# Sorting the keys of two batches with full-width products: two positions per product, all columns at once

## The chip, the cores and the metric

The kernel runs on one core of a Trainium2 chip. The metric is the device time of one execution in microseconds. Five engines matter. TensorE (PE in the profile) multiplies, with its weight loads shown as PEld. VectorE (DVE) and ScalarE (ACT) move results out of PSUM, the memory that TensorE writes. GpSimd (POOL) and SyncE (SP) mostly start transfers. A profile row names the line of the kernel, the engine, the operation, and the tiles as output<-input.

## The reference, cut to what matters

There are 4 batches, 8 heads, 768 positions and 64 columns per head. The positions of a head form 8 blocks of 96. A small matrix `P` per head (8 by 8) is normalised in five rounds; then blocks of keys and values are mixed by it, attention is computed inside each block, and the result goes through a two-layer network.

```python
k_sorted = np.einsum('bhij,bhjcd->bhicd', P, k_b)      # block i = sum over j of P[i, j] * block j
v_sorted = np.einsum('bhij,bhjcd->bhicd', P, v_b)
scores = scale * np.matmul(q_b, k_sb.transpose(0, 1, 2, 4, 3))
attn = softmax(scores)                                  # within a block of 96
x = (attn @ v_sb)                                       # heads side by side: 512 columns per token
r = np.maximum(x @ w_in, 0.0)                           # 512 -> 2048
out = (s * r * r + b) @ w_out                           # 2048 -> 512
```

The change touches only how `k_sorted` is made for batches 2 and 3.

## The kernel before, in words

Everything is written out by hand for one instruction stream per engine; there is no scheduler that reorders. Batches are worked on in halves of 384 tokens, numbered `t` = 0 to 7 (two per batch). For each half the network is `ffn1` (L464: 16 groups of 128 hidden columns, taken in pairs by `part`, products at L460, ReLU on ScalarE, squaring on VectorE) and `ffn2` (L478: three groups `m` of 128 tokens, each of 16 products at L484, and a move out by `store` on VectorE, L505). The loop at L618 runs, for each batch `b`, ffn1 of its two halves and then ffn2 of its two halves. The attention of the next batch `n = b + 1` is threaded between these products: dictionaries of slots name the pieces, and a piece's instructions are issued right after the product of its slot. In `ffn2`, slot `m * 4 + f // 4` comes after each four products.

The keys of batch `n` are sorted in `k_piece` (L290). The raw keys lie in SBUF with a partition for each (head, block, half of the block), 128 of them for the four pairs of heads, and (48 positions, 64 columns) along it. The matrices `P` of the batch form one table `PD[b]` with dimensions (partition, e, z, g): `e` is which head of a pair, `z` which half of a block, `g` the pair and the block, so 2 x 2 x 32 = 128 columns. A product for one position `c` and one `e` takes the 128 x 64 raw keys as weights and 64 columns of `PD` as the moving operand, and writes 64 partitions (the columns `d` of the keys) of PSUM: `e` = 0 to partitions 0 to 63, `e` = 1 to 64 to 127. So the two products of a position use two halves of TensorE's columns. A piece does 16 positions (CK), 32 products, and one move (`evac`, L202) of 1024 elements per partition on VectorE ("D") or ScalarE ("A") puts it in `KS`, whose last dimension is the position. Three pieces make a batch.

For batches 2 and 3 the three pieces are issued at once in slot 0 of `ffn2(2b)`, that is after the first four products of the first token group:

```python
            s0 = {0: [K(n, 0, "D"), K(n, 1, "A"), K(n, 2, "D")]}
        s1 = {0: [SC(n, 0, 0), SC(n, 0, 1)],
```

Their first use is by the scores (`SC`, `s_piece`, L353) in slot 0 of `ffn2(2b + 1)`. Batches 0 and 1 sort their keys elsewhere, with `k_piece` and `k_banks`, and are not touched.

PSUM tiles come from two pools in turn: `psa` (3 buffers of two banks: `hps` of ffn1, the sorted keys `tp`, scores, `pv`) and `psb` (2 buffers of one bank: `ops` of ffn2 and others). A product that opens a new tile waits until the tile that had the buffer before has been moved out. In `ffn2` the group `m` = 2 therefore needs the buffer that `store` of `m` = 0 has read.

Three transfers run in the background during this time: the sorted values come back through DRAM into `VS` (`v_back`, L339), the queries are transposed into `QT` by two transposing transfers on SP's queue (`q_dma`, L439), and finished rows go out (`store`). POOL's queue loads the raw keys of batch `n` before, in six parts (`load`, L86).

Of the kernel before, what the change touches and what calls it, by code (L numbers as in the profile page):

```python
# [9 lines left out]
FP = mybir.dt.float32  # L10
# [12 lines left out]
def kernel(  # L23
# [12 lines left out]
    nc = tc.nc  # L36

    B, H, S, D = q.shape
# [12 lines left out]
    NG = NHP * NB  # L51
    VW = D + 2
    CK = 16
# [15 lines left out]
    psa = ctx.enter_context(tc.tile_pool(name="psa", bufs=3, space=bass.MemoryType.PSUM))  # L69
# [14 lines left out]
    RAW = {}  # L84
# [37 lines left out]
    KS = [const.tile([128, NG, 2, GAP], BF, name=f"ks{i}") for i in range(2)]  # L122
# [79 lines left out]
    def evac(eng, out, in_):  # L202
        if eng == "A":
            nc.scalar.copy(out=out, in_=in_)
        else:
            nc.vector.tensor_copy(out=out, in_=in_)  # L206

    def q_banks(b, half, engs):
# [3 lines left out]
        for u in range(2):  # L212
# [13 lines left out]
            out=jsel, in_=ident.rearrange("p (h j z) -> p j h z", h=H, j=NB), axis=AX.XY, op=ALU.add),  # L226
        lambda: nc.vector.tensor_reduce(
            out=bm.rearrange("p (e z a) -> p e z a", e=2, z=2),
# [26 lines left out]
    PD = {}  # L255
# [34 lines left out]
    def k_piece(b, c0, eng):  # L290
        ps = psa.tile([128, CK, 2, NG], FP, tag="a", name="tp")
        for c in range(CK):
            for e in range(2):
                nc.tensor.matmul(out=ps[e * 64:(e + 1) * 64, c].rearrange("p z g -> p (z g)"),  # L294
                                 lhsT=RAW["k", b][:, c0 + c, :],
                                 rhs=PD[b][:, e].rearrange("p z g -> p (z g)"),
                                 start=True, stop=True)
        evac(eng, KS[b % 2][:, :, :, c0:c0 + CK], ps.rearrange("p c z g -> p g z c"))

    def k_banks(b, c0, engs):  # L300
        for u, eng in enumerate(engs):
            c1 = c0 + u * (CK // 2)
            ps = psb.tile([128, CK // 2, 2, NG], FP, tag="b", name="tkb")
            for c in range(CK // 2):
                for e in range(2):
                    nc.tensor.matmul(out=ps[e * 64:(e + 1) * 64, c].rearrange("p z g -> p (z g)"),
                                     lhsT=RAW["k", b][:, c1 + c, :],
                                     rhs=PD[b][:, e].rearrange("p z g -> p (z g)"),
                                     start=True, stop=True)
            evac(eng, KS[b % 2][:, :, :, c1:c1 + CK // 2], ps.rearrange("p c z g -> p g z c"))  # L310

    def v_piece(b, d0, eng, halves=None):
        ps = psa.tile([128, CK, 2 * NG], FP, tag="a", name="tv")
        for d in range(CK):
            for z in range(2):
                nc.tensor.matmul(out=ps[z * GAP:(z + 1) * GAP, d, :],  # L316
                                 lhsT=VP[b % 2][:, d0 + d, :], rhs=PD[b][:, :, z, :],
                                 start=True, stop=True)
        if halves is None:
            evac(eng, VS[b % 2][:, :, d0:d0 + CK], ps[0:KR].rearrange("p d g -> p g d"))  # L320
            return None

        def half(h, eng):
            hs = slice(h * HB, (h + 1) * HB)
            evac(eng, VS[b % 2].rearrange("p (g i) w -> p g i w", i=NB)[:, :, hs, d0:d0 + CK],
                 ps[0:KR].rearrange("p d (g i) -> p g i d", i=NB)[:, :, hs])

        half(0, eng)
        return lambda eng: half(1, eng)
# [23 lines left out]
    def s_piece(b, half, hp, sc=None):  # L353
        g0 = hp * NB + half * HB
        if sc is None:
            sc = psa.tile([128, 2, 512], FP, tag="a", name="sc")
        byp = len(QT[b].shape) == 5
        for n in range(HB):
            for e in range(2):
                pr = slice(e * 64, (e + 1) * 64)  # L360
                if byp:
                    o = sc[:, e, 0:TG].rearrange("p (c t) -> p c t", c=CQ)[:, :, 16 * n:16 * n + 16]
                    r = QT[b][pr, half, hp, :, 16 * n:16 * n + 16]
                else:
                    o = sc[:, e, n * BLK:(n + 1) * BLK]
                    r = QT[b][pr, half * HB + n, hp, :]
                nc.tensor.matmul(out=o, lhsT=KS[b % 2][pr, g0 + n].rearrange("p z c -> p (z c)"),  # L367
                                 rhs=r, start=True, stop=True)
        at = atp.tile([KR, 2, TG], BF, tag="at", name="at")
        if byp:  # L370
            nc.scalar.activation(out=at.rearrange("p e (t c) -> p e t c", c=CQ),
                                 in_=sc[0:KR, :, 0:TG].rearrange("p e (c t) -> p e t c", c=CQ),
                                 func=AF.Exp, scale=scale)
        else:
            nc.scalar.activation(out=at, in_=sc[0:KR, :, 0:TG], func=AF.Exp, scale=scale)  # L375
        AT[b, half, hp] = at

    def s_banks(b, half, hp):
        g0 = hp * NB + half * HB
        at = atp.tile([KR, 2, TG], BF, tag="at", name="at")  # L380
        sc = [psb.tile([128, TG], FP, tag="b", name="scb") for _ in range(2)]
        for n in range(HB):
            for e in range(2):
                pr = slice(e * 64, (e + 1) * 64)
                nc.tensor.matmul(  # L385
                    out=sc[e].rearrange("p (c t) -> p c t", c=CQ)[:, :, 16 * n:16 * n + 16],
                    lhsT=KS[b % 2][pr, g0 + n].rearrange("p z c -> p (z c)"),
                    rhs=QT[b][pr, half, hp, :, 16 * n:16 * n + 16], start=True, stop=True)
        for e in range(2):
            nc.scalar.activation(out=at[:, e].rearrange("p (t c) -> p t c", c=CQ),  # L390
                                 in_=sc[e][0:KR].rearrange("p (c t) -> p t c", c=CQ),
                                 func=AF.Exp, scale=scale)
        AT[b, half, hp] = at
# [119 lines left out]
    k_piece(0, 0, "D")  # L513
    k_piece(0, CK, "A")
    k_banks(0, 2 * CK, "DA")
    v_piece(0, 0, "D")
    sc1 = psa.tile([128, 2, 512], FP, tag="a", name="sc")
# [51 lines left out]
    def QF0(): return lambda: q_banks(0, 1, "AD")  # L569
    def SB(i): return lambda: s_banks(0, 1, i)  # L570
    def K(b, i, eng): return lambda: k_piece(b, i * CK, eng)
    def V(b, i, eng): return lambda: v_piece(b, i * CK, eng)
    def SC(b, h, i): return lambda: s_piece(b, h, i)
    def P(b, h, i): return lambda: p_piece(b, h, i)
# [3 lines left out]
    def TD(b, h): return lambda: t_dma(b, h)  # L578
# [5 lines left out]
    def halves(n):  # L584

        if n == 1:
            s0 = {4: [K(n, 0, "D"), K(n, 1, "A"), K(n, 2, "D")],
                  8: [V(n, 0, "D"), V(n, 1, "A"), V(n, 2, "D")],
                  10: [V(n, 3, "A")]}
        else:  # L590
            s0 = {0: [K(n, 0, "D"), K(n, 1, "A"), K(n, 2, "D")]}
        s1 = {0: [SC(n, 0, 0), SC(n, 0, 1)],
              3: [P(n, 0, 0), SC(n, 0, 2), SC(n, 0, 3)], 4: [P(n, 0, 1)], 5: [P(n, 0, 2)],
              6: [P(n, 0, 3), TD(n, 0), SC(n, 1, 0), SC(n, 1, 1)], 8: [P(n, 1, 0)],
              9: [P(n, 1, 1), SC(n, 1, 2), SC(n, 1, 3)], 10: [P(n, 1, 2)],
              11: [P(n, 1, 3), TD(n, 1)]}
        return s0, s1
# [15 lines left out]
    v_sort(1, range(4, 8))  # L613
    load("v", 2, 6, QT[1][:, NB - 1, 0, 0:1])
    s0, s1 = halves(1)
    ffn2(0, s0)
    ffn2(1, s1)
    for b in range(1, B):  # L618
        n = b + 1
        s0, s1, u0, u1 = {}, {}, {}, {}  # L620
        if n < B:
            load("k", n, 6, XT[2 * b + 1][:, HB - 1, NHP - 1, 0:1])
            load_q_rows(n)
            s0, s1 = halves(n)
            u0 = {i: [VRW(n, i)] for i in range(6)}
            u0[5] += [VB(n), QD(n)]
            if n + 1 < B:
                u0[5] += [LV(n + 1)]
        ffn1(2 * b, u0)
        ffn1(2 * b + 1, u1)  # L630
        ffn2(2 * b, s0)
        ffn2(2 * b + 1, s1)
# [30 lines left out]
```

## Time and profile before

| what | value |
|---|---|
| median of 3 runs | 224.14 us (224.11 to 224.17) |
| profiled execution | 224.16 us, of it the span 222.4 us |
| TensorE busy | 216.4 us, 97% of the span |
| VectorE / ScalarE / GpSimd busy | 119.7 / 99.3 / 70.4 us |
| TensorE clock granted | 1.0 (full) |
| sorting products of `k_piece` (L294), all batches | 352 products, weights 128x64, moving 64 columns |
| where batch 2 and batch 3 sort keys | from 102.44 us and from 151.37 us of the span |

A busy TensorE says little by itself, because its products overlap: a product of 326 ns in the table of groups is followed by the next one 162 ns later. What a product costs in a stream is the distance from its start to the next start. The chain of waits and the timeline give these: each line of the timeline has the start, the time until the group's last end, the engine, the operation, its shape and its count. A span given as "x4" from a start S covers four products.

### The profile page before, as it was taken

The numbers are of one execution on the slowest core, as the hardware profiler recorded it, in microseconds if no ns is written. First come the engines' busy times: TensorE is split into PE (matmuls) and PEld (weight loads), VectorE is DVE, ScalarE is ACT, GpSimd is POOL, SyncE is SP. The second block draws the span as 40 slices with busy tenths as digits, with TensorE's granted clock in tenths as the row PEclk, the third lists the DMA queues.
The fourth block names the chain that finished last, engine by engine and source line by source line (L and its number), as shares of the span: only waits on it lengthen the run. The fifth ranks groups of instructions, "written<-read, shape, count | busy, mean of one in ns | idle before, by whom it ended". The sixth has DMA issues, their size and how long they took to land.

```text
span 222.4 us, 5546 instructions
## 1 busy us (share of the span) xinstructions
PE 216.4 (97%) x2375; PEld 129.0 (58%) x2375; DVE 119.7 (54%) x243; ACT 99.3 (45%) x134; POOL 70.4 (32%) x127
## 2 busy tenths in 40 slices
PE   7989999999999999999999999999999999999993
PEld 5877766655655555666446555565445566554452
DVE  6777457559754768546216677446217744442121
ACT  4677687646244445664022534663024355650000
POOL 7659781679860004920032009700000000000000
PEclk9999999999999999999999999999999999999999
DMA  6999999999978432999989646999821440001212
GB/s 154 282 160 126 125 173 205 204 155 139 155 186 186 118 106 43 167 214 118 99 235 171 133 118 100 241 147 101 194 77 47 121 118 1 0 3 47 94 47 94
DMA packets 66936, 28.94 MB, mean 130 GB/s; under 512 B 51808, under 2 KB 62816, under 8 KB 66912
## 3 DMA queue, kind: packets, MB, share of 16 engines
q0 software_dynamic: 31168, 12.85, 49.2%
q1 hardware_dynamic: 35744, 15.74, 33.9%
q8 instruction: 18, 0.29, 0.6%
q14 instruction: 6, 0.05, 0.1%
HBM read 28.85 MB, written 7.86 MB: 165 GB/s over the span
## 4 chain that ended last, share of the span: by engine, by line
PE 91%; DMA 5%; DVE 1%; POOL 1%; issue 0%; ACT 0%; POOLq 0%
PE hps L460 38%; PE ops L484 37%; DMA rawk<-in_k_dram 5%; PE pv L409 4%; PE sc L367 3%; PE tp L294 2%; PE ops L497 2%; PE tv L316 2%; PE tvr L335 1%; DVE vs L206 1%; PE tr L426 1%; PE scb L385 1%; POOL rawk L93 0%; PE sc L259 0%; PE pv L403 0%; PE cps L559 0%
## 5 line engine op out<-in xcount | busy, mean ns | idle before, releaser
L460 PE MATMUL hps<-xt,wi 128*128 128x384 bf16 x512 | 87.9, 326 | 0.0
L484 PE MATMUL ops<-wo,gt 128*128 128x512 bf16 x368 | 85.0, 380 | 0.0
L472 ACT ACTIVATE rt<-hps 128x768 bf16<-128x768 f32 x64 | 51.8, 810 | 39.6 <-PE hps L460 38.9
L460 PEld LDWEIGHTS <-wi 128*128 128x128 bf16 x512 | 49.0, 98 | 32.6 <-issue 0.4
L473 DVE TENSOR_TENSOR gt<-rt 128x768 bf16<-128x768 bf16 x64 | 35.6, 558 | 41.2 <-ACT rt L472 41.0
L484 PEld LDWEIGHTS <-gt 128*128 128x128 bf16 x368 | 33.9, 98 | 37.3
L505 DVE SCALAR_TENSOR_TENSOR ot<-ops,s_bc,bias 128x512 f32<-128x512 f32 (+1 forms) x25 | 18.2, 729 | 42.7 <-PE ops L484 39.2
L375 ACT ACTIVATE at<-sc 112x768 bf16<-112x768 f32 x24 | 18.1, 807 | 41.3 <-PE sc L367 41.3
L415 DVE TENSOR_TENSOR x<-pv,rec 96x512 bf16<-96x512 f32 x32 | 22.0, 686 | 1.1
L116 POOL DMA_DIRECT2D qtok<-in_q_dram x24 | 18.6, 823 | 0.4 <-issue 0.4
L409 PEld LDWEIGHTS <-at 112*128 112x128 bf16 (+1 forms) x256 | 12.9, 101 | 6.7 <-ACT at L375 1.0
L142 POOL DMA_DIRECT2D wi<-in_moe_w_in_dram x24 | 12.8, 560 | 5.7 <-DMA rawk<-in_k_dram 3.0
L409 PE MATMUL pv<-vs,at 112*128 112x66 bf16 (+1 forms) x256 | 13.9, 195 | 0.1
L93 POOL DMA_DIRECT2D rawk<-in_k_dram x21 | 11.2, 554 | 3.7 <-issue 1.9
L93 POOL DMA_DIRECT2D rawv<-in_v_dram x18 | 9.7, 558 | 6.2 <-DMA wo<-in_moe_w_out_dram 5.1
L132 PE MATMUL z<-zeros 128*64 128x96 bf16 (+2 forms) x130 | 9.9, 243 | 1.2 <-DVE zeros L120 1.2
L90 POOL COPY rawk<-xt 128x1 bf16<-128x1 bf16 x2 | 0.4, 188 | 33.3 <-DMA xt<-x 33.3
L414 DVE RECIPROCAL rec<-pv 96x8 f32<-96x8 f32 x32 | 6.4, 200 | 6.4 <-PE pv L409 6.4
L132 PEld LDWEIGHTS <-zeros 128*64 128x64 bf16 (+1 forms) x130 | 7.6, 116 | 3.0 <-DVE zeros L120 1.2
L206 DVE CAST ks<-tp 128x1024 bf16<-128x1024 f32 x7 | 8.3, 1219 | 0.5 <-PE tp L294 0.3
L337 DVE CAST rawv<-tvr 128x512 bf16<-128x512 f32 x12 | 8.2, 684 | 0.0
L294 PEld LDWEIGHTS <-rawk 128*64 128x64 bf16 x352 | 6.0, 113 | 1.8 <-issue 1.3
(89 smaller groups left out, 134.5 us busy)
## 6 DMA issues: line engine op xcount, KB each, us to landing
out_dram<-ot SPq DMA_DIRECT2D x23, 256.0 KB, 2.4
rawv<-in_v_dram POOLq DMA_DIRECT2D x18, 128.0 KB, 5.4
rawk<-in_k_dram POOLq DMA_DIRECT2D x18, 128.0 KB, 4.4
qtok<-in_q_dram POOLq DMA_DIRECT2D x24, 96.0 KB, 6.4
wo<-in_moe_w_out_dram POOLq DMA_DIRECT2D x4, 512.0 KB, 11.1
v0f<-in_v_dram SPq DMA_DIRECT2D x4, 384.0 KB, 5.6
vd<-rawv SPq DMA_DIRECT2D x2, 768.0 KB, 6.2
vs<-vd SPq DMA_DIRECT2D x8, 192.0 KB, 7.7
```

The lines of the kernel that those rows point to most:

```text
L93: nc.gpsimd.dma_start(out=ti[:, c:c + n, :].rearrange("p c d -> p (c d)"), in_=raw["qkv".index(t)][b][:, c * D:(c + n) * D])
L116: nc.gpsimd.dma_start(out=ti[:, n + h], in_=qv[:, n + h])
L132: nc.tensor.matmul(out=z[0:m, 0:w], lhsT=zeros[:, 0:m], rhs=zeros[:, 0:w], start=True, stop=True)
L142: nc.gpsimd.dma_start(out=wi[:, al, f0:f1], in_=wiv[:, al, f0:f1])
L375: nc.scalar.activation(out=at, in_=sc[0:KR, :, 0:TG], func=AF.Exp, scale=scale)
L409: nc.tensor.matmul(out=pv[0:m, e, n * VW:(n + 1) * VW], lhsT=atf[:, c0:c0 + m], rhs=VS[b % 2][:, e * NG + g0 + n, :], start=True, stop=True)
L415: nc.vector.tensor_tensor(out=x[:, :, hp * 128:(hp + 1) * 128].rearrange("p n (e d) -> p e n d", e=2), in0=pvv[:, :, :, 0:D], in1=rec.unsq ...
L460: nc.tensor.matmul(out=H1[t, i][:, f, 0:TG], lhsT=wi[:, hp, fc:fc + 128], rhs=XT[t][:, :, hp, :], start=(hp == 0), stop=(hp == NHP - 1))
L472: nc.scalar.activation(out=rt, in_=h, func=AF.Relu)
L473: nc.vector.tensor_tensor(out=gt[:, 2 * i:2 * i + 2, :], in0=rt, in1=rt, op=ALU.mult)
L484: nc.tensor.matmul(out=ops, lhsT=gt[:, f, m * 128:(m + 1) * 128], rhs=wo[:, f, :], start=(f == 0), stop=(f == NF - 1))
L505: nc.vector.scalar_tensor_tensor(out=ot[:, ns], in0=ops, scalar=s_bc, in1=BIAS[0][:, ns], op0=ALU.mult, op1=ALU.add)
```

## The change

`k_pairs` replaces `k_piece` for batches 2 and 3. It takes two neighbouring positions as one set of weights (2 x 64 = 128 columns) and all 128 columns of `PD[b]` as the moving operand. A piece of 16 positions is then 8 products that write all 128 partitions. PSUM holds, for a pair of positions, position `u` = 0 on partitions 0 to 63 and `u` = 1 on 64 to 127, with both heads `e` side by side along the partition; `KS` wants the heads on the two halves of the partitions and the positions side by side. So a piece is moved out in four copies of 64 partitions x 512 elements: two for `e` = 0 on VectorE, then two for `e` = 1 on ScalarE, each writing every second position of its 16.

```diff
+    def k_pairs(b, c0):
+        m = CK // 2
+        ps = psa.tile([128, m, 2, 2 * NG], FP, tag="a", name="tpp")
+        for j in range(m):
+            nc.tensor.matmul(out=ps[:, j].rearrange("p e g -> p (e g)"),
+                             lhsT=RAW["k", b][:, c0 + 2 * j:c0 + 2 * j + 2, :].rearrange(
+                                 "p c d -> p (c d)"),
+                             rhs=PD[b].rearrange("p e z g -> p (e z g)"), start=True, stop=True)
+        for e in range(2):
+            for u in range(2):
+                evac("DA"[e],
+                     KS[b % 2][e * 64:(e + 1) * 64, :, :, c0 + u:c0 + CK:2],
+                     ps[u * 64:(u + 1) * 64, :, e].rearrange("p c (z g) -> p g z c", z=2))
...
+    def KP(b, i): return lambda: k_pairs(b, i * CK)
...
-            s0 = {0: [K(n, 0, "D"), K(n, 1, "A"), K(n, 2, "D")]}
+            s0 = {0: [KP(n, 0), KP(n, 1), KP(n, 2)]}
```

## The prediction

> **What bounds the kernel now.** I read the busy line of the page first, then the chain of work that ended last, to see whether TensorE's stream is also the path that sets the end.
>
> ```profile
> PE 216.4 (97%) x2375; PEld 129.0 (58%) x2375; DVE 119.7 (54%) x243; ACT 99.3 (45%) x134; POOL 70.4 (32%) x127
> PE 91%; DMA 5%; DVE 1%; POOL 1%; issue 0%; ACT 0%; POOLq 0%
> ```
>
> TensorE is on the chain for 91% of the span, and the 5% of DMA is one load at the very start. From 20.7 us to 219 us every piece of the chain is TensorE's. So a microsecond taken out of TensorE's stream there is a microsecond off the end, unless something that TensorE waits for becomes late.
>
> Next I read the chain around the place of the change, batch 2 (columns: start, us on the chain, what):
>
> ```profile
> 101.65 0.86 PE ops L484 x4
> 102.51 1.64 PE tp L294 x96
> 104.15 10.46 PE ops L484 x48
> 114.62 0.45 PE sc L367 x16
> ```
>
> The 96 sorting products of a batch hold the path for 1.64 us (batch 3, from 151.44, the same). The 48 products behind them take 10.46, while 48 at the usual distance (0.86 / 4 = 0.216) would be 10.37: the stream loses about 0.09 at the seam. The starts in the timeline of TensorE show both seams; three narrow windows around them gave these lines:
>
> ```profile
> 102.13 0.38 PE L484 MATMUL ops<-wo,gt 128*128 128x512 bf16 x1
> 102.44 0.22 PE L294 MATMUL tp<-pd,rawk 128*64 128x64 bf16 x1
> 104.08 0.39 PE L484 MATMUL ops<-wo,gt 128*128 128x512 bf16 x1
> ```
>
> The last `ops` product before starts at 102.13, the first sorting product 0.31 later, which is 0.09 over 0.216. From 102.13 to the next `ops` start at 104.08 are 1.95 us. That is the whole price of the piece of stream that the change replaces. Does the loss at the seams come from the half-width form, or from a wait? The stream of batch 1 has the comparison, first in starts:
>
> ```profile
> 75.66 0.81 PE L484 MATMUL ops<-wo,gt 128*128 128x512 bf16 x3
> 76.30 0.43 PE L409 MATMUL pv<-vs,at 112*128 112x66 bf16 x8
> 76.67 0.51 PE L367 MATMUL sc<-qt,ks 64*128 64x96 bf16 x16
> ...
> 77.99 0.43 PE L409 MATMUL pv<-vs,at 112*128 112x66 bf16 x8
> 78.25 1.03 PE L484 MATMUL ops<-wo,gt 128*128 128x512 bf16 x4
> ```
>
> The third `ops` product starts at 75.66 + 2 x 0.216 = 76.09, and `pv`, whose weights fill all columns, follows 0.21 later: no loss. Eight `pv` take 0.37 before `sc` (weights on half of the rows, 64*128) and 0.26 before `ops`: entering a split form costs 0.11. The way out is seen on the chain, where the four `ops` behind `sc` and the four behind `pv` stand as
>
> ```profile
> 77.18 0.97 PE ops L484 x4
> ...
> 78.42 0.87 PE ops L484 x4
> ```
>
> so leaving the split form costs 0.10. The boundaries at `pv` carry semaphore waits too, so the loss goes with the split form and not with the wait.
>
> **The change part by part.**
>
> *Removed: 96 half-width products a batch, 1.95 us from the last `ops` start to the next one.*
>
> *Added: 24 products with 128x128 weights and 128 moving columns.* The trace has this shape: the fillers at L455.
>
> ```profile
> L455 PEld LDWEIGHTS <-zeros x5: 95/98/99, 23.1 to 23.6; 128*128 128x128 bf16 x5
> 23.30 0.17 PE hps L455 x3
> 23.80 0.11 PE hps L455 x2
> ```
>
> Three take 0.17 on the chain and two 0.11: 0.056 each, each with its own weight load of 98 ns that is hidden. A second way to the number: on the chain eight `hps` products of 384 moving columns take 1.30, 0.1625 each, and one `ops` of 512 takes 0.216, that is 0.0535 for 128 more; 0.1625 - 2 x 0.0535 gives 0.0555 for 128. I take 0.056. The new stretch is one `ops` distance and 24 products with no seam: 0.216 + 24 x 0.056 = 1.56. Gain 1.95 - 1.56 = 0.39 a batch; the next `ops` behind a split form also comes a little late (the 0.09 of the 48 and the seams of 0.09 and 0.10 are rounded to 0.01), and I take 0.40. With 0.40 in each of two batches the gain is 0.80.
>
> [...]
>
> *Moves out.* Before: VectorE 2 x 1219 ns, ScalarE 1 x 1012 ns a batch. After: VectorE six copies and ScalarE six, of 512 elements on 64 partitions, and ScalarE's two of each piece wait for VectorE's two of it. The nearest rows:
>
> ```profile
> L206 DVE CAST ks<-tkb 128x512 bf16<-128x512 f32 x1 | 0.7, 692 | 0.1
> L204 ACT CAST ks<-tkb 128x512 bf16<-128x512 f32 x1 | 0.6, 585 | 0.0
> L196 ACT CAST vp<-v0f 128x768 bf16<-128x768 f32 x4 | 5.9, 1510 | 0.0
> L204 ACT COPY qt<-tqb 128x768 bf16<-128x768 bf16 x2 | 1.6, 788 | 0.0
> ```
>
> Fewer partitions save nothing (112x1024 and 128x1024 casts take 1218 and 1219). The new part is writing every second bf16, which no row shows. Below: 692 and 585, since nothing in the change makes a copy shorter. Above: the widely strided read of `vp` costs 1510 against 788 for as many elements in line, a factor 1.92, which makes 1.33 and 1.12 us. I take the lower end: the same rows already gather from PSUM with a stride, and a step of one element is nearest to the copies in line. [...]
>
> What hides them: VectorE is free from 102.53 + 0.56 = 103.09. Six copies end at 103.09 + 6 x 0.692 = 107.24, and queued behind them is `store` of `m` = 0 (0.75), done at 107.99 instead of 107.63. TensorE needs that buffer when `m` = 2 opens, 28 products after the sort: 104.08 + 28 x 0.216 + 0.01 = 110.14 before, 109.74 now. Cover 1.75 us. ScalarE ends two copies after VectorE's last, 107.24 + 1.17 = 108.41; `KS` is needed by the scores at 114.56 - 0.40 = 114.16. Cover 5.7 us; ScalarE has nothing else to do until then. Both are costed at nothing; past its cover, each microsecond of VectorE or ScalarE is a microsecond of TensorE. SP issues the output row of `m` = 0 only after its transposes, at 112.38, so the later `store` delays no transfer.
>
> *What TensorE reaches earlier.* The scores wait for the first half of `QT`, whose transfer does not move with TensorE:
>
> ```profile
> 106.41 5.88 SPq L443 DMA_TRANSPOSE qt<-qtok  x2
> DMA to landing us min/median/max: 4.3/5.5/6.6
> ```
>
> Landed by 106.41 + 6.6 = 113.0 at the latest, needed at 114.16: 1.15 us of cover (batch 3: issued at 152.01, landed by 158.3, needed near 162.7). The sorted values land by 102.28 + 10.9 = 113.2, needed by the first `pv` at 117.60 - 0.40 = 117.2. The raw keys land by 94.6 (last issue 89.1, at most 5.5 to landing), needed at 102.4. No DMA is added or moved past a queue.
>
> **Sum.** 224.16 (profiled, span 222.4 and 1.76 around it) - 0.80 = 223.36; the median of the runs is 0.02 below the profiled one, so 223.34.
>
> **Rivals.**
>
> 1. *Slower: VectorE's interleaved writes.* If a copy costs 1.33, the sixth ends at 111.07 and `store` at 111.82, 2.08 after `m` = 2 wants the buffer; less the gain of 0.40 that is 1.68 a batch, 227.5. The stall begins above 0.98 us a copy, and from 1.05 it eats the gain ((110.14 - 0.75 - 103.09) / 6). For it: the doubled ScalarE row. Against: that row reads elements 64 apart.
> 2. *Slower: products bound by their weight loads.* At 98 ns each the stretch is 0.216 + 24 x 0.098 = 2.57, +0.62 a batch, 225.4. It decides from 72 ns a product on. Against: fillers at 56, and `pv` every 33 ns with 98 to 101 ns loads.
> 3. *The seams stay.* If the 0.19 of both seams is a price of this place and not of the split form, the gain is 0.21 a batch, and the time 223.72. Against: `pv`.
> 4. *A late `QT` swallows batch 2's gain.* It needs the first transposes 1.55 us later than here; 223.74.
> 5. *The change does not do what it says.* The built stream of the changed kernel has 24 weight loads and 24 products of 128x128 in place of the 96 in each batch, and nothing else moved on TensorE, so I give this nothing beyond 1 in 100: 224.14.
>
> **How the numbers follow.** Forecast 0.78; rival 1 0.06, rival 2 0.04, rival 3 0.08, rival 4 0.03, rival 5 0.01. About 0.2% (0.45 us) is what a measurement of this kernel can tell from no change. The forecast lies beyond it (0.36%), rivals 3 to 5 within it, rivals 1 and 2 on the other side: faster 0.78, same 0.12, slower 0.10. The forecast's own range, for 0.055 to 0.060 a product, is 223.3 to 223.55. The range 223.15 to 223.85 adds rivals 3 and 4 and a little on the fast side.
>
> **What would show it.** Right: from the last `ops` start to the next 1.56 us, starts 0.056 apart, 0.22 before the first of them; no idle time of TensorE before the third `ops` group or the scores. VectorE's six copies near 0.69 each, ending near 107.2. Wrong: copies over 1 us with a gap before `m` = 2; starts more than 0.07 apart; a gap of 0.1 at either seam; a gap before the first `sc`.

## The result, and the profile after

The changed kernel takes 223.45 us (median of 10 runs, 222.92 to 223.82) against 224.12 for the kernel before (10 runs); the ratio is 0.9965 with a 95% interval of 0.995 to 0.998. It is faster by 0.67 us. The forecast was 223.34. Of all runs in this document one, of `p6_batch1_too` (228.31 us), was over 1.5% above the fastest of its kernel and is left out of that kernel's median and ratio. The profiled execution took 223.59 us with a span of 221.8.

The busy line and the chain's shares by engine, from the page of the changed kernel:

```profile
PE 214.8 (97%) x2212; PEld 129.6 (58%) x2231; DVE 123.3 (56%) x251; ACT 106.1 (48%) x144; POOL 70.6 (32%) x127
PE 95%; DVE 2%; issue 1%; ACT 0%
```

TensorE is the chain still; VectorE and ScalarE are busy for 3.6 and 6.8 us more, and none of their copies of these keys stands on the chain (VectorE's 2% of it are work of the start-up and the last `store`). The chain around batch 2 (start, us, what):

```profile
102.15 0.59 PE ops L498 x2
102.75 1.34 PE tpp L304 x24
104.09 4.96 PE ops L498 x23
109.05 0.05 issue
109.10 5.34 PE ops L498 x24
114.45 0.45 PE sc L381 x16
```

The sort holds the path for 1.34 us instead of 1.64, and the products behind it show no seam: 4.96 / 23 = 0.216. (The "issue" of 0.05 is the place of one product whose record is missing: 47 are listed, 48 were done, and the piece is 10.35 long.) The starts on TensorE's timeline at the two seams:

```profile
102.15 0.59 PE L498 MATMUL ops<-wo,gt 128*128 128x512 bf16 x2
102.58 0.22 PE L304 MATMUL tpp<-pd,rawk 128*128 128x128 bf16 x1
103.92 0.38 PE L498 MATMUL ops<-wo,gt 128*128 128x512 bf16 x1
```

The second `ops` starts at 102.15 + 0.22 = 102.37, the first paired product 0.21 later, the next `ops` at 103.92: 1.55 to 1.56 us in place of 1.95.

The moves, by tile (nanoseconds least/median/most), and VectorE's timeline behind them:

```profile
L206 DVE CAST ks<-tpp x12: 719/728/742, 103.2 to 155.5; 64x512 bf16<-64x512 f32 x12
L204 ACT CAST ks<-tpp x12: 721/724/733, 104.8 to 157.1; 64x512 bf16<-64x512 f32 x12
```

```profile
103.24 4.46 DVE L206 CAST ks<-tpp 64x512 bf16<-64x512 f32 x6
107.74 0.75 DVE L519 SCALAR_TENSOR_TENSOR ot<-ops,s_bc,bias 128x512 f32<-128x512 f32 x1
```

VectorE's copies end at 107.70, `store` of `m` = 0 at 108.49, and TensorE opens `m` = 2 near 109.97 without a wait. ScalarE's six copies of each batch end near 109.2 and 157.8, some 5 us ahead of the scores.

**The same work in every run, and the rest.** To see how much of a run's time the change governs, take the stretch from the first `cps` product (the bias, done once, just before batch 1's keys) to the last `store`. On the chain of the kernel before, and of the changed one, these two points are:

```profile
45.27 0.98 PE cps L559 x16
219.00 0.48 DVE ot L505
```

```profile
45.50 0.98 PE cps L573 x16
218.44 0.48 DVE ot L519
```

That is 173.73 us before and 172.94 after: 0.79 shorter, where the forecast said 0.80. The span is only 0.6 shorter in these two executions because the changed kernel's reached `cps` 0.23 later. The code ahead of that point is the same in both.

### The profile page after: what moved, and what is told of

Same layout as the page of the kernel before. It is cut to its first block, busy times and chain, and to the rows that moved or that the text cites. A ratio compares the mean times of both kernels' runs of the same rounds, so it can differ in the third digit from the quotient of the medians.

```text
span 221.8 us, 5257 instructions
## 1 busy us (share of the span) xinstructions
PE 214.8 (97%) x2212; PEld 129.6 (58%) x2231; DVE 123.3 (56%) x251; ACT 106.1 (48%) x144; POOL 70.6 (32%) x127
## 4 chain that ended last, share of the span: by engine, by line
PE 95%; DVE 2%; issue 1%; ACT 0%
PE hps L474 38%; PE ops L498 36%; PE z L132 5%; PE pv L423 4%; PE sc L381 3%; PE ops L511 2%; PE tv L330 2%; PE tp L294 1%; PE tpp L304 1%; PE tvr L349 1%; DVE vs L206 1%; PE tr L440 1%; PE scb L399 1%; PE sc L259 0%; PE pv L417 0%
## 5 line engine op out<-in xcount | busy, mean ns | idle before, releaser
L498 PE MATMUL ops<-wo,gt 128*128 128x512 bf16 x350 | 82.4, 379 | 1.5 <-issue 0.8
L132 PE MATMUL z<-zeros 128*64 128x96 bf16 (+2 forms) x129 | 10.8, 257 | 1.3 <-DVE zeros L120 1.2
L204 ACT CAST ks<-tpp 64x512 bf16<-64x512 f32 x12 | 8.7, 725 | 4.4 <-DVE ks L206 4.1
L132 PEld LDWEIGHTS <-zeros 128*64 128x64 bf16 (+1 forms) x130 | 8.5, 128 | 3.0 <-DVE zeros L120 1.2
L206 DVE CAST ks<-tpp 64x512 bf16<-64x512 f32 x12 | 8.7, 728 | 0.2
```

The lines of the kernel that those rows point to most:

```text
L132: nc.tensor.matmul(out=z[0:m, 0:w], lhsT=zeros[:, 0:m], rhs=zeros[:, 0:w], start=True, stop=True)
L498: nc.tensor.matmul(out=ops, lhsT=gt[:, f, m * 128:(m + 1) * 128], rhs=wo[:, f, :], start=(f == 0), stop=(f == NF - 1))
```

## The experiments

All of them stand on a base of their own, in which the twelve transposing transfers are plain transfers of the same bytes; for each, the stretch from `cps` to the last `store` is read from its trace, since it has shown itself steadier than the whole time.

| run | edit | median, us (runs) | stretch, us |
|---|---|---|---|
| p0_before | base, kernel before | 224.08 (12) | 173.74 |
| p1_after, p1_after_2 | base, changed kernel | 222.93 (6), 222.92 (5) | 172.94, 172.95 |
| p2_batch2_only | pairs in batch 2 alone | 223.51 (12) | 173.34 |
| p3_full_n64 | all weight columns, half the moving ones | 223.25 (12) | 173.06 |
| p4_moves_all_vector | all copies on VectorE | 230.07 (4) | 180.4 |
| p8_moves_all_scalar | all copies on ScalarE | 223.29 (4) | 172.93 |
| p5_in_line | copies write in line | 223.54 (1) | 172.94 |
| p6_batch1_too | pairs in batch 1 too, old slots | 225.85 (4) | 176.6 |
| p7_batch1_later_v, _2 | pairs in batch 1, values later | 222.82 (9), 222.91 (6) | 172.44, 172.44 |

### The base, and the change on it

```diff
-        nc.sync.dma_start_transpose(out=xt..., in_=x...)
+        nc.sync.dma_start(out=xo[0:BLK], in_=xi[:, 0:NHP * HB * BLK])
+        nc.sync.dma_start(out=xo[BLK:128], in_=xi[0:128 - BLK, 0:NHP * HB * BLK])
...
```

(and the same for the queries; `xo`, `xi` are the two tiles with all but the partitions flattened).

> The kernel before with its twelve transposing transfers (queries and attention output) replaced by plain transfers of the same bytes, two for each; it leaves out the transposition, so the data behind it are not the reference's. All engines' work and its order are the same. It is the base for the experiments below. Such transfers land in a few us as the transposing ones do and TensorE waited for none of those, so 224.1 (224.0 to 224.3).

> The changed kernel on the same base (plain transfers, the transposition left out). Theory A: the change saves 0.80 us of TensorE's stream behind the start-up, and what remains of the spread between runs is the start-up, which the change does not touch. Then the time is 0.80 below the base, 223.3; in the profile the last ops start to the next is 1.56 us against 1.95 in both batches, and the stretch from the 36 hps products behind the last tr of batch 0 to the last move out is 0.80 shorter than in the base. Theory B: part of the saving is lost again further on (0.67 is the difference of the medians on record), and that stretch is 0.6 to 0.7 shorter.

> The changed kernel on the base once more, beside the next one on the same chip. If the changed stretch is fixed and the start-up alone varies, the stretch from the cps products to the last store is again 172.9 us (172.94 in the first run), and the median lies between 222.7 and 223.6, as the start-up falls.

Measured: the base is at 224.08 us against 224.07 for the kernel before on that chip (ratio 1.0003, 0.9991 to 1.0015), with a stretch of 173.74 against 173.73: a fair stand-in. The changed kernel on it has ratios of 0.9948 (0.9933 to 0.9963) and 0.9943 (0.993 to 0.9956), and stretches of 172.94 and 172.95. So the stretch falls by 0.79 to 0.80 us each time (theory A), to a hundredth as forecast. The whole time fell by 0.67 in the result and by 1.15 here, to 0.37 below the 223.3 that were expected. In the profiled executions the time behind the last `store` is the same with the change and without it (2.9 us in the result, 2.6 on the base), and the start-up makes the difference: with the change `cps` began 0.23 us later in the result and 0.10 earlier here (45.13 against 45.23).

### One batch at a time

```diff
-            s0 = {0: [KP(n, 0), KP(n, 1), KP(n, 2)]}
+            s0 = {0: [KP(n, 0), KP(n, 1), KP(n, 2)] if n == 2 else
+                  [K(n, 0, "D"), K(n, 1, "A"), K(n, 2, "D")]}
```

> On the same base (the transposition left out): paired products for batch 2 alone, batch 3 as before. If each batch saves its 0.40 us on its own, the time is 0.40 below the base and 0.40 above the changed one: 223.7. If the gain of one batch is swallowed by a later wait, it is 223.3 or 224.1.

Measured: stretch 173.34, exactly half way; median 223.51, 0.57 below the base and 0.58 above the changed kernel, where 0.40 was forecast for each. Each batch saves 0.40 us of the stretch on its own, and nothing is taken back between them.

### Seams or fewer products

```diff
-            nc.tensor.matmul(out=ps[:, j].rearrange("p e g -> p (e g)"), lhsT=<2 positions>,
-                             rhs=PD[b].rearrange("p e z g -> p (e z g)"), start=True, stop=True)
+            for e in range(2):
+                nc.tensor.matmul(out=ps[:, j, e], lhsT=<2 positions>,
+                                 rhs=PD[b][:, e].rearrange("p z g -> p (z g)"), start=True, stop=True)
```

(`<2 positions>` stands for the weights of two neighbouring positions, written out in the change above.)

> On the same base (the transposition left out): weights over all 128 columns as in the changed kernel, but the moving operand cut into its two halves of 64 columns, 48 products a batch instead of 24, same PSUM layout and same moves. Theory A: the seams of 0.09 and 0.10 us belong to the form that splits the columns, so they are gone here too. With pv's 33 ns a product the stretch is 0.216 + 48 x 0.033 = 1.80 us, 0.24 longer than 1.56: 0.48 above the changed kernel, 223.8. Theory B: the seams belong to short products or to the place: the stretch is 1.80 + 0.19 = 1.99, no gain over the base, 224.1 to 224.2.

TensorE's timeline of this run, from three windows:

```profile
103.41 0.59 PE L502 MATMUL ops<-wo,gt 128*128 128x512 bf16 x2
103.84 1.56 PE L305 MATMUL tpp<-pd,rawk 128*128 128x64 bf16 x48
105.45 0.38 PE L502 MATMUL ops<-wo,gt 128*128 128x512 bf16 x1
```

The second `ops` starts at 103.63 and the first sorting product 0.21 later, so the entry seam is gone though the moving operand is as short as before. The first record of `ops` behind the sort is missing here; the one listed is the second, so the first started near 105.24, 0.03 behind the last sorting product (105.21): no exit seam either. (The scores start 10.24 us behind the listed `ops`, against 10.46 behind the first one in the changed kernel, which is one product more.) The sort's stretch is 1.61 (0.216 more in the lines). Over the whole stretch this form costs 0.12 more than the changed kernel, 0.06 a batch, and saves 0.34 of the 0.40. Theory A holds: the seams go with the split columns. Its price was too high: a product of 64 moving columns takes 1.40 / 48 = 0.029 us here, not the 0.033 taken from `pv` with its 66 columns. So of the 0.40, about 0.20 are the seams, about 0.06 come from having 24 products instead of 48, and most of the rest, 0.12, from the slower rhythm of the split pairs: in the kernel before a pair starts every 0.0317 us, here a product every 0.0291.

### What hides the moves

```diff
-                evac("DA"[e],
+                evac("D",        # p4; "A" in p8
```

> On the same base (the transposition left out): all twelve copies of a batch on VectorE. They tell what lies behind the cover: store of m = 0 is queued behind them, and the group m = 2 of ffn2 opens its PSUM buffer only after it. Twelve copies of 0.728 from 103.24 (start in the changed kernel) end at 111.98, store at 112.73, and m = 2 wants the buffer at 103.92 + 28 x 0.216 = 109.97: a wait of 2.8 us a batch, 5.5 above the changed kernel on this base (222.93), 228.4. If the buffer were not what limits and only the scores need the copies (114.4), nothing changes: 222.9.

> On the same base (the transposition left out): all twelve copies of a batch on ScalarE, the mirror of the run with all on VectorE, which cost 6 to 8 us. Twelve of 0.724 from about 103.2 end near 111.9; the scores need them at 114.4, ScalarE has nothing else before, and store of m = 0 is free on VectorE. If the cost of that run came from the store queued behind the copies, and not from the amount of copying, nothing is lost here: the stretch from the cps products to the last store is 172.9 us. If the late copies themselves delay the scores, it grows by up to 2 us a batch.

With all copies on VectorE, its timeline and TensorE's in batches 2 and 3:

```profile
103.20 8.84 DVE L206 CAST ks<-tpp 64x512 bf16<-64x512 f32 x12
112.07 1.41 DVE L522 SCALAR_TENSOR_TENSOR ot<-ops,s_bc,bias 128x512 f32<-128x512 f32 x2
```

```profile
112.88 6.02 PE L501 MATMUL ops<-wo,gt 128*128 128x512 bf16 x20 [2.79 <-DVE ot L522]
...
165.89 4.48 PE L501 MATMUL ops<-wo,gt 128*128 128x512 bf16 x20 [2.78 <-DVE ot L522]
```

The waits are those that were worked out, 2.79 and 2.78 us, released by `store`, at the opening of `m` = 2. (Counted from start to start each costs 2.95: the product before it starts at 109.71, the one behind at 112.88, instead of 0.216 later.) The cover is real and it is this buffer. The time is worse than forecast (230.07 for 228.4; ratio 1.026, 1.0225 to 1.0295), and the two lines say why: the same 20 products took 6.02 us after the first wait and 4.48 after the second. Twice 2.95 and this 1.54 make the 7.4 us by which the stretch is longer than the changed kernel's. The stages behind each (columns: window; sum, then PE, PEld, DVE, ACT, POOL busy; granted clock; DMA):

```profile
113.00:115.00 2.00, 2.00 (x6) 0.62 (x5) 0.48 (x1) 0.00 (x0) 0.61 (x2) 0.50 0.67 249
115.00:117.00 2.00, 2.00 (x8) 0.80 (x7) 0.00 (x0) 0.00 (x0) 2.00 (x5) 0.74 0.64 92
...
166.00:168.00 2.00, 2.00 (x10) 0.88 (x9) 0.50 (x1) 0.00 (x0) 0.00 (x0) 1.00 0.64 240
```

After the first wait the granted clock was 0.50, then 0.74; after the second it stayed 1.00. The four runs fall in two groups: two near 229.0 with a mean granted clock of 1.000, which is 6.1 above the changed kernel, and two near 231.0 with 0.992 and 0.993. The profiled execution is of the second group.

With all copies on ScalarE nothing is lost in the stretch: 172.93, ratio 0.9952 (0.9937 to 0.9968). (The median, 223.29, is 0.37 above the changed kernel's on that chip; in the profiled executions `cps` began 0.62 later, at 45.70 against 45.08.) The same amount of copying ends as late, and the scores still find it done:

```profile
103.43 8.88 ACT L204 CAST ks<-tpp 64x512 bf16<-64x512 f32 x12 [0.50 <-PE tpp L304]
114.96 1.51 ACT L389 ACTIVATE at<-sc 112x768 bf16<-112x768 f32 x2 [2.65 <-PE sc L381]
```

It is not the copying that costs; it is what stands in the queue behind it.

### Why a copy takes 728 and 724 ns

```diff
-                     KS[b % 2][e * 64:(e + 1) * 64, :, :, c0 + u:c0 + CK:2],
+                     KS[b % 2][e * 64:(e + 1) * 64, :, :, c0 + u * m:c0 + (u + 1) * m],
```

> As the changed kernel on the same base (the transposition left out), but each copy writes eight positions in line instead of every second of sixteen; this leaves out the right order of the positions inside a group of 16 keys as well. It tells why a copy takes 728 ns on VectorE and 724 on ScalarE and not 692 and 585 as the nearest rows. If the step of the write is the reason, the copies fall to about 692 and 585. If it is the step of the read from PSUM (128 elements between positions instead of 64) or the half of the partitions, they stay at 728 and 724. The stretch from the cps products to the last store stays 172.9 us either way, since the copies are hidden.

The moves by tile in this run:

```profile
L206 DVE CAST ks<-tpp x12: 674/688/694, 103.4 to 155.5; 64x512 bf16<-64x512 f32 x12
L204 ACT CAST ks<-tpp x12: 577/578/582, 104.9 to 156.9; 64x512 bf16<-64x512 f32 x12
```

In line they cost what the nearest rows said (692 and 585). Writing every second position adds 40 ns on VectorE (6%) and 146 on ScalarE (25%); the step of the read and the half of the partitions add nothing. The stretch is 172.94: hidden either way.

### The same edit where the cover is short

```diff
-            s0 = {4: [K(n, 0, "D"), K(n, 1, "A"), K(n, 2, "D")],
+            s0 = {4: [KP(n, 0), KP(n, 1), KP(n, 2)],
                   8: [V(n, 0, "D"), V(n, 1, "A"), V(n, 2, "D")],
                   10: [V(n, 3, "A")]}
```

> On the same base (the transposition left out): the paired form for batch 1 too, in its old slots. There the sort of the values opens its PSUM tiles 16 products behind the keys, and VectorE is busy with the first store until 58.0. Theory A (the cover decides): VectorE's copies end tile by tile at 59.5, 60.9, 62.4 and ScalarE's, behind them, at 60.9, 62.4, 63.8; the third tile of the values wants its buffer near 60.4, so TensorE waits about 3 us there less the 0.40 saved: 225.5 to 226.0 (2.6 to 3.0 above the changed kernel on this base). Theory B (the form pays wherever it is put): 222.5.

TensorE's timeline in batch 1:

```profile
59.63 0.69 PE L330 MATMUL tv<-pd,vp 128*64 128x64 bf16 x32 [0.45 <-ACT ks L204]
61.12 0.69 PE L330 MATMUL tv<-pd,vp 128*64 128x64 bf16 x32 [0.79 <-ACT ks L204]
62.61 0.98 PE L330 MATMUL tv<-pd,vp 128*64 128x64 bf16 x32 [0.80 <-ACT ks L204]
63.52 3.20 PE L501 MATMUL ops<-wo,gt 128*128 128x512 bf16 x8
```

Each third of the values' sort waits for ScalarE's copies of the keys, 2.0 us together (3 were expected; VectorE's copies began 1.4 us earlier than in the trace that the working used). And again the clock went: eight `ops` take 3.20 instead of 1.9, in stages of which the windows say

```profile
62.00:64.00 2.00, 1.39 (x34) 1.05 (x34) 1.29 (x2) 1.58 (x2) 2.00 (x5) 0.69 0.75 124
64.00:66.00 2.00, 2.00 (x6) 0.68 (x5) 0.85 (x1) 0.00 (x0) 0.30 (x1) 0.50 1.25 223
```

Ratio to the kernel before 1.0058 (1.0036 to 1.008): the edit that pays in batches 2 and 3 costs 3.7 us of the stretch here, in a profiled execution with a mean clock of 0.992. Two runs with 0.999 and 1.000 took 224.83 and 225.39, about 2.2 above the changed kernel. Theory A, with a part that it did not have: the median lies in its range (225.5 to 226.0), but from less waiting than it had and, in half of these four runs, a lower clock that it did not have.

### A version with the cover made

```diff
-            s0 = {4: [K(n, 0, "D"), K(n, 1, "A"), K(n, 2, "D")],
-                  8: [V(n, 0, "D"), V(n, 1, "A"), V(n, 2, "D")],
-                  10: [V(n, 3, "A")]}
+            s0 = {4: [KP(n, 0, "AD"), KP(n, 1, "AD"), KP(n, 2, "AD")],
+                  10: [V(n, 0, "D"), V(n, 1, "A"), V(n, 2, "D")]}
...
-        s1 = {0: [SC(n, 0, 0), SC(n, 0, 1)],
+        s1 = {0: [V(n, 3, "A")] * (n == 1) + [SC(n, 0, 0), SC(n, 0, 1)],
```

("AD" means that ScalarE takes the first head and VectorE the second.)

> On the same base (the transposition left out): batch 1 in pairs with the cover made. ScalarE, free since 54, takes the first head of each piece and VectorE the second; the three first pieces of the values are issued two slots later (10 instead of 8), and the fourth directly ahead of the first scores, where the stream is split already. VectorE's last copy ends near 62.4, the third tile of the values wants its buffer near 62.1. Theory A: the sort saves 0.40, one pair of seams goes as well (about 0.1 to 0.2), and some tenths of waiting remain: the stretch from the cps products to the last store is 172.3 to 172.8 us instead of 172.9, faster than both kernels on this base. Theory B: the waiting at the values or at the first scores eats it: 173 or more.

> The version with batch 1 in pairs and later values, once more beside the changed kernel. The first run's stretch was 172.44 against 172.94. If that is its gain, the stretch is 172.4 again and the median about 0.5 below the kernel beside it; the start-up of either can blur up to some tenths of that.

TensorE's timeline in batch 1 has no wait left:

```profile
55.23 1.50 PE L304 MATMUL tpp<-pd,rawk 128*128 128x128 bf16 x24
56.57 5.34 PE L501 MATMUL ops<-wo,gt 128*128 128x512 bf16 x24
61.84 1.71 PE L330 MATMUL tv<-pd,vp 128*64 128x64 bf16 x96
63.49 1.90 PE L501 MATMUL ops<-wo,gt 128*128 128x512 bf16 x8
65.32 0.69 PE L330 MATMUL tv<-pd,vp 128*64 128x64 bf16 x32
65.94 0.52 PE L381 MATMUL sc<-qt,ks 64*128 64x96 bf16 x16
```

The stretch is 172.44 in both runs, 0.50 below the changed kernel on this base and 1.30 below the base. Of the 0.50, batch 1's sort gives 0.39 (from the `ops` start ahead of it to the next at 56.57 are 1.56 us, 1.95 in the kernel before); the rest, about 0.10, fits the pair of seams that is merged, and no run has it alone. The ratios to the kernel before are 0.9952 (0.9933 to 0.9971) and 0.9946 (0.9925 to 0.9966). Beside the changed kernel on the same chip, the medians (222.91 and 222.92) do not tell the two apart, though about 0.5 between them was forecast; only the stretch does. It was run on the base with plain transfers alone.

## Why the prediction was right, step by step

- **The sum.** 0.40 a batch and 0.80 in all: the stretch fell by 0.79 to 0.80 in the result and on the base, and by 0.40 with one batch. The median fell by 0.67 and 1.15, on both sides of it. That the result came within 0.11 us of the forecast is in part luck of the start-up: a fall of 1.15 would have put it at 222.99, below the range. What is confirmed is the stretch.
- **The price of a product.** 24 products at 0.056 us: the sort is on the chain for 1.34 = 24 x 0.056, with weight loads of 98 ns each. So the products did not come at the pace of their weight loads, and rival 2 fell.
- **The seams.** That they belong to the split columns was argued from `pv` and `sc`, and the run with full columns and short products shows it: both seams are gone there. Rival 3 fell.
- **The moves.** Here a term was mis-sized: "I take the lower end" gave 692 and 585 ns; they were 728 and 724. The step that failed was to call writing every second bf16 nearest to writing in line. It cost nothing, as the cover of VectorE shrank from the 1.75 us worked out to about 1.5 (`store` ended at 108.49 and not 107.99).
- **Rival 1's mechanism** is the right one with the wrong price: the buffer behind `store` does decide when VectorE has more to do (2.79 us of waiting where 2.8 were worked out), but a copy would have to cost over 0.98 us, and costs 0.73.
- **A late `QT`.** On the chain the scores start right behind the last `ops` product, with no wait, at 114.45; rival 4 did not occur. That `QT` could be made late on purpose was not tried.
- **Not in the prediction:** the start-up. In the profiled executions `cps` began between 45.1 and 46.75 us, with the same code ahead of it. The products on zeros that TensorE does first (`warm`, L132) show one way. In the same window the kernel before and the changed one did (columns as above):

```profile
6.00:8.00 2.00, 2.00 (x51) 2.00 (x49) 1.67 (x9) 0.76 (x2) 1.88 (x6) 1.00 1.16 310
```

```profile
6.00:8.00 2.00, 2.00 (x37) 2.00 (x36) 1.67 (x9) 0.76 (x2) 1.89 (x6) 1.00 1.15 311
```

51 products against 37 of the same line: TensorE reached its full rhythm later. From 4.8 us on these products start 0.080 us apart, in the first execution up to 5.2 us and in the second up to 7.2, and 0.042 apart from there. (The clock of 1.00 in both lines does not show this: the first clock record of the two traces stands only at 5.17 and 7.17.) So the first product with real data started at 11.96 instead of 11.23. The kernel before then waited for a load of raw keys at 14.49 and gave back most of that lead. In eight of the profiled executions, these two among them, 37 to 52 such products stand between 6 and 8 us. With 51 or 52 of them there and 29 or more between 4 and 6, the first real product follows at 11.22 or 11.23 (three executions); with 50 or 51 there and 20 or 21 between 4 and 6, at 11.38 and 11.41 (two); with 37 to 43 there, at 11.93 to 11.96 (three). And one and the same kernel, `p7_batch1_later_v`, reached `cps` at 46.09 and, in its second run, at 45.21. So the start-up differs from execution to execution. Whether a changed instruction stream shifts the start-up on average, so that 0.67 and 1.15 both have a reason beyond chance, is left open.

## What to carry to other kernels

Where TensorE's stream is the path, count a piece of it from the start of the product before it to the start of the product behind it: half of what this change saved lay in the two seams, and a table of durations shows neither. Here the cheaper form on TensorE was paid for with more and dearer moves (twelve copies a batch, 8.7 us together, for three of 3.45), and whether they were hidden depended on which engine's queue they stood in and what waited behind them: the same twelve copies a batch cost nothing on ScalarE and about 6 us a kernel on VectorE, 7.4 with the half clock behind one wait. In the stage with less cover the same edit lost about 2 us against the changed kernel, 3.7 with a half clock, until the consumer was moved back and the idle engine took the first copies.

## What the runs showed that was not expected

In two traces a wait of TensorE went with a loss beyond its length. In the run with all copies on VectorE the granted clock was 0.95 from 109 to 113 us, 0.50 from 113 to 115 and 0.74 from 115 to 117: by an estimate from these three, about 3.4 us at 0.50, from 112.6 to 116.0. Behind the wait of 2.79 us six products stand in the 2 us from 113 to 115; behind the equal wait of 2.78, at a clock of 1.00, ten stand in those from 166 to 168. The 20 products behind the first wait took 1.54 us more. Three shorter waits (0.45, 0.79, 0.80) in batch 1 came with a lower clock as well: 0.69 from 62 to 64, 0.50 from 64 to 66 and 0.95 from 66 to 68, again about 3.4 us at 0.50. That the waits are the cause is not shown: one of the twelve runs of the base (225.30 us, not profiled) has a mean clock of 0.991, and the profiled execution of the base has no such waits. Nor does the length of a wait separate the cases: 2.79 us, and 2.04 in three parts, came with the lower clock, 2.78 did not. What decides is left open; no run changed the length or the place of a wait alone.

Writing every second bf16 cost ScalarE's copies a quarter more time and VectorE's 6% (724 against 578, 728 against 688 ns).
